# Feed-forward input products of 512 columns, with the last 64 rows of four batches in shared products

## The chip, the cores and the metric

One core of one Trainium2 chip runs the whole program. The metric is the device time of one execution in microseconds (us), as the median of several runs. TensorE is called PE here, VectorE DVE, ScalarE ACT, GpSimd POOL and SyncE SP. Each takes its own instructions in order and waits for the others by semaphores.

## The reference

Eight attention heads for four batches of 576 rows, with a learned bias, feed a gated feed-forward part:

```python
scores = scale * q @ k.T + bias            # bias from log distances, a small two-layer net
attn = exp(scores - max); attn /= sum + 1e-09
x = (attn @ v)                             # per batch 576 x 512 (8 heads of 64)
h = np.maximum(x @ w_in, 0.0)              # 512 -> 1024
conv_out = sum of conv_w[k] * h shifted by k-1 rows, k = 0, 1, 2
gate = 1.0 / (1.0 + np.exp(-conv_out))
out = h * gate @ w_out                     # 1024 -> 512
```

## The kernel before

The attention part (about the first 280 us) goes through 16 pairs of heads and batches, `seq`, with the pair of heads as the outer loop and the batch as the inner one. Its result stands transposed in `xb[b]`: 128 partitions (features of one pair) by 4 pairs by 576 rows. The last pair of all is the fourth of batch 3 (n = 15). The sums of its softmax go from SBUF through DRAM back to all partitions (`store_sums`, `spread_sums`, tile `rb`, both issued by POOL), and `apply_norm` on POOL (L511) multiplies them in.

The feed-forward part works with numbers split into two parts, a rounded high one and the rest (`split_x`, L133 and L134 on POOL), so that each product of matrices is three products: high by high, high by low, low by high. `x_parts(b, c)` splits the quarter c of `xb[b]` into the tile `xs`; `wi` holds w_in and `wo` w_out in the same form. The rows of a batch are columns of the products.

`ffn_in(b, f)` (L529 to L549) makes the hidden features 128 f to 128 f + 127 of batch b: 4 quarters by 3 products by two halves of 288 columns, 24 matmuls at L536, into one of two PSUM tiles (`psS`), from which ACT takes the positive part into `h` (L548). Then four stages follow for each f: `tap` (the middle weight of the convolution; on ACT at L763 for batch 0, on DVE at L761 for the others), `conv` (two DVE instructions at L768), `gate` (a tanh on ACT at L774, then DVE at L775), and `g_parts` (ACT rounds the high part at L90, DVE subtracts for the low part at L788; 512 columns go to a tile `g`, the last 64 to `gt[f]`, which two batches share). The stages are laid out as a pipeline of sets: set j holds conv of f = j-1, gate of j-2, g_parts of j-3 and tap of j. In the loop over `steps` the set j is written right behind `ffn_in(b, j)`, and three more sets drain the pipe. So the first gate of a batch is written behind f = 2.

After the eight f of a batch, `x_parts(b + 1, c)` is written, held back by a dependency until DVE has done the low part of f = 6 (`gated[b, FC - 2]`). Then `ffn_out` (L793) multiplies by w_out: for each f four row tiles of 128 rows, 3 products of 512 columns each, 12 matmuls. For batches 1 and 3 a fifth group does the 64 last rows of two batches together from `gt`, in batch 3 as two halves of 256 columns. In batch 3 the f from 4 on are done row tile by row tile, so that tiles can be stored one by one.

The products for f = 0 and 1 of batch 0 are placed between the last attention units. `wo` for f = 6 and 7 is made in the feed-forward part: DVE and ACT narrow the raw 64-bit words (L99, L101, L105), POOL splits them.

Between engines the order of writing is the order of each engine's queue; nothing reorders it.

Of the kernel before, what the change touches and what calls it, by code (L numbers as in the profile page):

```python
# [9 lines left out]
F32 = mybir.dt.float32  # L10
F32R = mybir.dt.float32r
# [8 lines left out]
def attention_ffn_kernel(  # L20
# [35 lines left out]
    def halves(ap):  # L56
        return ap.rearrange("p (a b) -> p a b", a=2)
# [11 lines left out]
    psum = {"s": psE, "tp": psB, "o": psB}  # L69
    raw_p = pool(ctx, "raw", 2)  # L70
    w_p = pool(ctx, "w", KC + 1)
    x_p = pool(ctx, "x", B)
    e_p = pool(ctx, "e", 2)
    woe_p = pool(ctx, "woe", 1)
    FE = 6

    ident = const.tile([P, P], F32, name="ident")
# [59 lines left out]
    with tc.manual_schedule():  # L137
# [55 lines left out]

        SW = 2 * (S + 32)
        ybuf = [w_p.tile([P, 3, S], F32, name=f"y{i}", tag="w") for i in range(KC)]
        x0 = x_p.tile([P, NP, S], F32, name="x0", tag="x")
        y3 = x_p.tile([P, 4, S], F32, name="y3", tag="x")
        tl = x_p.tile([P, SW + tabs.shape[1]], F32, name="tl", tag="x")
        st1 = x_p.tile([P, SW], F32, name="st1", tag="x")
# [111 lines left out]
        pty_p = pool(att, "pty", 1)  # L311
        sm_p = pool(att, "sm", 4)
        r_p = pool(att, "r", 2)
        rb_p = pool(att, "rb", 1)

        rr_t = [vz_p.tile([P, P], F32, name=f"rr{i}") for i in range(2)]
        for r in rr_t:
# [201 lines left out]
        def x_parts(b, c):  # L519
            if c % 2 == 0:  # L520
                xss["raw"] = raw_p.tile([P, 2, 2, S], F32R, name="xs", tag="raw")
            xs = xss["raw"][:, c % 2]
            first = split_x(xs, xb[b][:, c])
            if b and c == 0:
                tc.add_manual_dep(first.ins, gated[b - 1, FC - 2].ins.name, mybir.DependencyInfo(
                    mybir.DependencyClass.Sync, mybir.DependencyReason.DATA))
            xss[b, c] = xs

        def ffn_in(b, f):  # L529
            ps = psS.tile([P, 2, 512], F32, name="s")  # L530
            cs = slice(f * P, f * P + P)
            i = 0
            for c in range(KC):
                for pw, px in ((0, 0), (0, 1), (1, 0)):
                    for a in range(2):
                        nc.tensor.matmul(  # L536
                            ps[:, a, 0:HS],
                            wi[c][:, pw, cs],
                            xss[b, c][:, px, a * HS:(a + 1) * HS],
                            start=(i == 0),  # L540
                            stop=(i == 3 * KC - 1),
                        )
                    i += 1
            if (b, f) in ((0, 0), (0, 1)):
                h = e_p.tile([P, S], F32, name="h")
            else:
                h = g_p[0].tile([P, S], F32, name="h", tag="g")
            nc.scalar.activation(halves(h), ps[:, :, 0:HS], AF.Relu)  # L548
            return h  # L549

        cwr = []

# [16 lines left out]

        def load_wo(f):  # L570
            if not raw_o:
                raw_o.append(x_p.tile([P, 2, DM, 2], I32, name="raw_o", tag="x"))
            load_w(raw_o[0][:, f % 2], w_out[f * P:(f + 1) * P, :])

        conv_weights = {68: load_conv, 71: narrow_conv, 73: turn_conv}
# [84 lines left out]
        for u, (n, t) in enumerate(flat):  # L660
# [29 lines left out]
            del spt[n, t]  # L690
            if u + 2 >= NU:
                f = u + 2 - NU
                hs_ff[0, f] = ffn_in(0, f)
            if u in (2, 4) or n > 1 and ui == 2 and n + 2 < NSEQ:
                load(n + 2 if n > 1 else 2 + u // 4)
            if u in conv_weights:
# [44 lines left out]
        apply_norm(NSEQ - 2)  # L741
        store_sums(NSEQ - 1)
        spread_sums(NSEQ - 1)
        apply_norm(NSEQ - 1)
        att.close()


# [1 line left out]
        wo_p = pool(ff, "wo", 1)  # L749
        g_p[0] = pool(ff, "g", FC + 4)  # L750
        e2_p = pool(ff, "e2", 2)
        wc_p = pool(ff, "wc", 2)
        o_p = pool(ff, "oo", 3)

        wo += [wo_p.tile([P, 2, DM], F32R, name=f"wo{f}") for f in range(FE, FC)]
# [67 lines left out]
            if k == 3:  # L823
                g_parts(b, f, cvs.pop((b, f)))

        for i, (b, f) in enumerate(steps):
            if b == 0 and f in (2, 4):
                c = FE - 1 + f // 2
                split_w(wc_p, wo[c], raw_o[0][:, c % 2])
            if (b, f) not in hs_ff:  # L830
                hs_ff[b, f] = ffn_in(b, f)
            for k in (1, 2, 3, 0):
                if k <= f:
                    stage(i - k, k)
            if f < FC - 1:
                continue
            for j in range(3):
                for k in (1, 2, 3):
                    if k > j:
                        stage(i + 1 + j - k, k)  # L840
            for c in range(KC):
                if b + 1 < B:
                    x_parts(b + 1, c)
            po = [psT.tile([P, 512], F32, name="tp") for _ in range(3)]
            po.append(psO.tile([P, 512], F32, name="o"))
            lhs = [
                lambda f, gi, t=t: gs[b, f][:, gi, t * P:(t + 1) * P] for t in range(NT)
            ]
            both = FC if b + 1 < B else FC // 2
            for f in range(both):  # L850
                for t in range(NT):
                    ffn_out(po[t], lhs[t], [f])
            for t in range(NT):
                ffn_out(po[t], lhs[t], range(both, FC))
                store(po[t], out[b, t * P:(t + 1) * P, :], t % 2)
            if b % 2:

                nh = 1 if b + 1 < B else 2
                for k in range(nh):
                    cs = slice(k * DM // nh, (k + 1) * DM // nh)  # L860
                    pt = psT.tile([P, 512], F32, name="tp")[:, 0:DM // nh]
                    ffn_out(pt, lambda f, gi: gt[f][:, gi], range(FC), cs)
                    store(pt, out[b - 1:b + 1, NM:, cs], k)
# [82 lines left out]
```

## Time and profile before

| what | value |
|---|---|
| median of 3 runs | 491.34 us (490.48 to 491.41) |
| the profiled execution: its time | 491.75 us |
| the profiled execution: its span | 489.9 us |
| PE busy | 474.1 us, 97% |
| DVE, ACT, POOL busy | 364.3, 311.8, 147.8 us |
| mean granted clock of PE | 0.996 of 2.4 GHz |

The span is the time from the first to the last instruction of the profiled execution; its time holds 1.85 us more. A row of the timeline gives the start and the length of a group of instructions of one kind, and in square brackets the time the engine sat idle ahead of it and what ended that. Matmuls overlap: the length of one is longer than the distance from one to the next, and the distance is what counts in a sum.

### The profile page before, as it was taken

To read this page: it belongs to the slowest core of one execution; us is meant where nothing else is said; L and a number is where in the kernel's file an instruction comes from. 1 tells how busy PE (TensorE), PEld (TensorE's weight loads), DVE (VectorE), ACT (ScalarE), POOL (GpSimd) and SP (SyncE) were. 2 spreads that over 40 slices of the span, in tenths; PEclk is the share of its full clock that TensorE was granted. 3 is DMA by queue.
4 is the path that set the end of the run, shared out by engine and by line. 5 is a ranking of instruction groups with operands and counts; after the bars stand their busy time and mean duration, and the time that the engine had idled before them with its cause. 6 is when DMAs were issued, how large, how long until landed. Compare 5 with 4: busy or idle time off the path is not lost.

```text
span 489.9 us, 11074 instructions
## 1 busy us (share of the span) xinstructions
PE 474.1 (97%) x4202; PEld 352.5 (72%) x4202; DVE 364.3 (74%) x871; ACT 311.8 (64%) x751; POOL 147.8 (30%) x215
## 2 busy tenths in 40 slices
PE   6988899999999999999999999999999999999996
PEld 4333356666666666666666789889988999899986
DVE  6999976788898889988898729944891279438930
ACT  5999886898888889888888836712550145124510
POOL 1000001355445835465457725160007000600000
PEclk9989999999999999999999999999999999999999
DMA  1899857598668795579751300002000200020011
GB/s 37 229 340 301 339 161 164 138 271 221 158 183 208 218 249 156 159 208 272 211 131 50 111 26 26 2 0 87 0 1 1 107 1 1 1 86 1 1 44 64
DMA packets 32584, 60.82 MB, mean 124 GB/s; under 512 B 7196, under 2 KB 15796, under 8 KB 32532
## 3 DMA queue, kind: packets, MB, share of 16 engines
q1 hardware_dynamic: 27380, 47.02, 33.0%
q0 software_dynamic: 4768, 12.77, 9.0%
q8 instruction: 33, 0.54, 0.5%
q10 hardware_dynamic: 384, 0.35, 0.2%
q14 instruction: 19, 0.16, 0.1%
HBM read 44.12 MB, written 15.98 MB: 123 GB/s over the span
## 4 chain that ended last, share of the span: by engine, by line
PE 85%; DVE 0%; issue 0%; DVEq 0%
PE s L536 21%; PE o L471 18%; PE s L363 16%; PE tp L793 16%; PE tp L434 9%; PE o L793 4%; PE s L422 1%; PE s L426 0%; DVE pty L93 0%; DVE sp L374 0%; DVE o L801 0%; PE tp L491 0%; DVE ptx L93 0%; PE tp L565 0%; DVEq L801 0%
## 5 line engine op out<-in xcount | busy, mean ns | idle before, releaser
L374 DVE CUSTOM_DVE_ANT_0 sp<-s,bt 128x576 f32<-128x576 f32 x144 | 103.9, 753 | 30.0 <-PE s L363 12.2
L388 ACT ACTIVATE sp<-sp,nm 128x576 f32<-128x576 f32 x144 | 109.9, 767 | 0.0
L536 PEld LDWEIGHTS s<-xs,wi 128*128 128x128 f32 x768 | 102.8, 189 | 1.2 <-issue 0.5
L536 PE MATMUL s<-xs,wi 128*128 128x288 f32 x768 | 103.6, 296 | 0.0
L363 PE MATMUL s<-qk 64*128 64x288 f32 (+1 forms) x640 | 93.0, 431 | 2.8 <-DVE nm L374 2.1
L363 PEld LDWEIGHTS s<-qk 64*128 64x128 f32 (+1 forms) x640 | 46.8, 175 | 44.3 <-DVE nm L374 15.1
L793 PE MATMUL tp<-wo,g 128*128 128x512 f32 x288 | 70.1, 389 | 0.0
L434 PE MATMUL tp<-identr,sr 64*128 64x64 f32 x1184 | 64.3, 247 | 1.8 <-ACT sp L388 1.8
L793 PEld LDWEIGHTS tp<-wo,g 128*128 128x128 f32 x288 | 53.8, 188 | 11.0
L434 PEld LDWEIGHTS tp<-identr,sr 64*128 64x128 f32 x1184 | 55.6, 136 | 8.0 <-ACT sp L388 2.4
L548 ACT ACTIVATE h<-s 128x576 f32<-128x576 f32 x32 | 20.9, 652 | 55.2 <-PE s L536 55.1
L768 DVE SCALAR_TENSOR_TENSOR cv<-h,cw,cv 128x575 f32<-128x575 f32 x64 | 52.6, 821 | 2.5 <-ACT cv L763 0.6
L250 DVE TENSOR_SCALAR y<-tl,inv,nb 128x576 f32<-128x576 f32 (+33 forms) x112 | 47.6, 498 | 0.1
L471 PE MATMUL o<-ptx,vt 128*64 128x320 f32 x300 | 46.8, 442 | 0.0
L267 PE MATMUL s<-y,pars 128*32 128x512 f32 (+8 forms) x352 | 43.0, 530 | 1.3 <-DVE y L250 0.7
L471 PE MATMUL o<-pty,vt 128*64 128x256 f32 x320 | 44.2, 393 | 0.0
L133 POOL TENSOR_SCALAR xs<-x 128x576 fp32r<-128x576 f32 x16 | 11.9, 743 | 94.9 <-DVE gt L788 94.8
L803 ACT ACTIVATE o<-tp 128x512 f32<-128x512 f32 (+1 forms) x10 | 5.8, 577 | 51.7 <-PE tp L793 51.7
L498 POOL DMA_DIRECT2D r_d<-rt x16 | 10.0, 625 | 87.5 <-DVE rt L93 87.5
L267 PEld LDWEIGHTS s<-y,pars 128*32 128x32 f32 x352 | 16.5, 118 | 25.2 <-DVE y L250 8.2
L801 DVE TENSOR_SCALAR o<-tp 128x512 f32<-128x512 f32 (+1 forms) x5 | 3.2, 638 | 39.6 <-PE tp L793 39.6
L93 DVE COPY ptx<-tp 128x256 f32<-128x256 f32 (+1 forms) x64 | 32.0, 499 | 0.6 <-PE tp L434 0.4
(83 smaller groups left out, 666.1 us busy)
## 6 DMA issues: line engine op xcount, KB each, us to landing
qk<-in_qk_dram SPq DMA_DIRECT2D x32, 320.0 KB, 5.2
bias_d<-st SPq DMA_DIRECT2D x13, 607.0 KB, 5.8
bt<-bias_d POOLq DMA_DIRECT2D x24, 288.0 KB, 6.5
qk<-in_qk_dram SPq DMA_DIRECT2D x32, 144.0 KB, 5.5
rb<-r_d POOLq DMA_DIRECT2D x32, 144.0 KB, 3.2
vt<-in_v_dram SPq DMA_DIRECT2D x16, 256.0 KB, 6.0
raw_w<-in_moe_w_in_dram SPq DMA_DIRECT2D x16, 256.0 KB, 4.7
out_dram<-o SPq DMA_DIRECT2D x16, 256.0 KB, 2.0
```

What stands on the lines that cost most here:

```text
L93: nc.vector.tensor_copy(o, i)
L250: nc.vector.tensor_scalar(y, dist[:, 0:n], inv[:, ig:ig + 1], nb1, op0=ALU.mult, op1=ALU.max)
L267: nc.tensor.matmul(ps[32 * j:32 * j + 32, a // 512 if n > 512 else blk % 2, 0:min(n - a, 512)], w2b, ys[j][:, a:min(n, a + 512)], start=Tr ...
L363: nc.tensor.matmul(ps[po, a, 0:HS], qt[rows, qo:qo + po.stop - po.start], qt[rows, KO + hh * HS:KO + hh * HS + HS], start=True, stop=True,)
L374: nc.vector.tensor_tensor_reduce(out=halves(spt[n, t][0][:, h]), in0=ps[:, :, 0:HS], in1=halves(bt[:, h]), op0=ALU.add, op1=ALU.min, scale ...
L388: exps[n, t, h] = nc.scalar.activation(sp[:, h], sp[:, h], AF.Exp, bias=nm[:, h:h + 1], scale=-1.0, accum_out=sms[n][:, col:col + 1],)
L434: tr = nc.tensor.transpose(ps[a][:, TL * s:TL * s + TL].bitcast(F32R), spf[ra, j:j + P], identr[ra, ra])
L471: nc.tensor.matmul(po[D * h:D * h + D, 0:width], vt[:, slot, :], pt[:, blk, :], start=(c == 0), stop=(c == 4),)
L536: nc.tensor.matmul(ps[:, a, 0:HS], wi[c][:, pw, cs], xss[b, c][:, px, a * HS:(a + 1) * HS], start=(i == 0), stop=(i == 3 * KC - 1),)
L548: nc.scalar.activation(halves(h), ps[:, :, 0:HS], AF.Relu)
L768: nc.vector.scalar_tensor_tensor(out=cv[:, o:o + S - 1], in0=h[:, i:i + S - 1], scalar=cw[:, f, kk:kk + 1], in1=cv[:, o:o + S - 1], op0=AL ...
L793: nc.tensor.matmul(ps, lhs(f, gi), wo[f][:, wj, cs], start=(f == 0 and i == 0), stop=(f == FC - 1 and i == 2),)
```

## The change

The input products of a batch take its first 512 rows in one product instead of 576 rows in two halves. The last 64 rows of all four batches are gathered in a tile `xr` (quarter, high or low, batch, row), and `ffn_rest` makes one product of 256 columns for all of them. These pooled products are written in batch 0, behind its own wide products: f = 6, then pooled 0, f = 7, pooled 1, and then the pooled ones in pairs. ACT takes the 64 columns of batch 0 into `h` and the 192 columns of the others into `hr[f]`; in batches 1 to 3 it copies 64 columns from `hr[f]` into `h`. `x_rest(0)` fills `xr` by DVE from `xs`, `x_rest(1..3)` by POOL from `xb[b]`; for batch 3 that is behind `apply_norm` of the last pair, which moves behind the split of `wo` for f = 6 and two of these. The sets of the gate pipeline of batch 0 are written behind the pooled products (`run`); in batches 1 to 3 three sets go with four f, so that the first gate is written behind f = 3. In batch 3 the row tiles part at f = 6 instead of 4. Some tiles change their pools.

```diff
         def x_parts(b, c):
...
+            n = NM if b else S
             xs = xss["raw"][:, c % 2]
-            first = split_x(xs, xb[b][:, c])
+            first = split_x(xs[:, :, 0:n], xb[b][:, c, 0:n])
...
+        def x_rest(b):
+
+            if b == 0:
+                for k in range(2):
+                    dve(xr[0][:, 2 * k:2 * k + 2, :, 0], xss[0, "pair", k][:, :, :, NM:])
+                return
+            x, hi, lo = xb[b][:, :, NM:], xr[0][:, :, 0, b], xr[0][:, :, 1, b]
+            nc.gpsimd.tensor_scalar(hi, x, 1.0, 0.0, op0=ALU.mult, op1=ALU.add)
+            nc.gpsimd.tensor_sub(lo, x, hi.bitcast(F32))
+
+        xr, hr = [], []
+
+        def in_products(ps, f, rhs):
             i = 0
             for c in range(KC):
                 for pw, px in ((0, 0), (0, 1), (1, 0)):
-                    for a in range(2):
-                        nc.tensor.matmul(
-                            ps[:, a, 0:HS],
-                            wi[c][:, pw, cs],
-                            xss[b, c][:, px, a * HS:(a + 1) * HS],
-                            start=(i == 0),
-                            stop=(i == 3 * KC - 1),
-                        )
+                    nc.tensor.matmul(
+                        ps, wi[c][:, pw, f * P:f * P + P], rhs(c, px), start=(i == 0), stop=(i == 3 * KC - 1)
+                    )
                     i += 1
+
+        def ffn_in(b, f, ps=None):
+
+            if ps is None:
+                ps = psS.tile([P, 2, 512], F32, name="s")
+            in_products(ps[:, 0], f, lambda c, px: xss[b, c][:, px, 0:NM])
...
-            nc.scalar.activation(halves(h), ps[:, :, 0:HS], AF.Relu)
-            return h
+            nc.scalar.activation(h[:, 0:NM], ps[:, 0], AF.Relu)
+            if b:
+                act(h[:, NM:], hr[f][:, b - 1])
+            hs_ff[b, f] = h
+
+        def ffn_rest(ps, f):
+            in_products(ps[:, 0:B * TL], f, lambda c, px: xr[0][:, c, px].rearrange("p b s -> p (b s)"))
+            nc.scalar.activation(hs_ff[0, f][:, NM:], ps[:, 0:TL], AF.Relu)
+            nc.scalar.activation(hr[f].rearrange("p b s -> p (b s)"), ps[:, TL:B * TL], AF.Relu)
...
         spread_sums(NSEQ - 1)
-        apply_norm(NSEQ - 1)
         att.close()
...
-        for i, (b, f) in enumerate(steps):
-            if b == 0 and f in (2, 4):
-                c = FE - 1 + f // 2
-                split_w(wc_p, wo[c], raw_o[0][:, c % 2])
-            if (b, f) not in hs_ff:
-                hs_ff[b, f] = ffn_in(b, f)
-            for k in (1, 2, 3, 0):
-                if k <= f:
-                    stage(i - k, k)
-            if f < FC - 1:
-                continue
-            for j in range(3):
-                for k in (1, 2, 3):
-                    if k > j:
-                        stage(i + 1 + j - k, k)
+        def run(b, sets):
+            for j in sets:
+                for k in (1, 2, 3, 0):
+                    if 0 <= j - k < FC:
+                        stage(b * FC + j - k, k)
+
+        hr += [hr_p.tile([P, B - 1, TL], F32, name=f"hr{f}") for f in range(FC)]
+        ws = [narrow(tp, raw_o[0][:, k], ("cv", "cv")) for k, tp in enumerate((e_p, e2_p))]
+        xr.append(xa_p.tile([P, KC, 2, B, TL], F32R, name="xr", tag="x"))
+        x_rest(0)
+        split_x(wo[FE], ws[0])
+        for b in range(1, B):
+            if b == B - 1:
+                apply_norm(NSEQ - 1)
+            x_rest(b)
+        split_x(wo[FE + 1], ws[1])
+
+        for b in range(B):
+            if b == 0:
+                for f in range(2, 6):
+                    ffn_in(0, f)
+                for j, todo in enumerate(((6, None, 0), (7, None, 1), (None, 2, 3), (None, 4, 5), (None, 6, 7))):
+                    main, *rest = todo
+                    ps = psS.tile([P, 2, 512], F32, name="s")
+                    if main is not None:
+                        ffn_in(0, main, ps)
+                    for k, f in enumerate(rest):
+                        if f is not None:
+                            ffn_rest(ps[:, k], f)
+                    run(0, [j])
+                done = 5
+            else:
+                done = 0
+                for f in range(FC):
+                    ffn_in(b, f)
+                    upto = (3 * f + 1) // 4 + 1
+                    run(b, range(done, upto))
+                    done = upto
+            run(b, range(done, FC + 3))
...
-            both = FC if b + 1 < B else FC // 2
+            both = FC if b + 1 < B else 3 * FC // 4
```

PE's queue before, from the last input products of batch 0 (f = 7) into its first output products; `s` is the PSUM tile, `wi_751` to `wi_754` are the four quarters of w_in:

```order
L536 MATMUL s<-xs,wi_751 128x288 x6
L536 MATMUL s<-xs,wi_752 128x288 x6
L536 MATMUL s<-xs,wi_753 128x288 x6
L536 MATMUL s<-xs,wi_754 128x288 x6
L793 MATMUL tp<-wo_755,g 128x512 x9
L793 MATMUL o<-wo_755,g 128x512 x3
```

PE's queue of the change at the same place, from the products of f = 6 on; the rows with `xr` are pooled products, and six more such groups (f = 2 to 7) follow the last row:

```order
L548 MATMUL s<-xs,wi_757 128x512 x3
L548 MATMUL s<-xr,wi_754 128x256 x3
L548 MATMUL s<-xr,wi_755 128x256 x3
L548 MATMUL s<-xr,wi_756 128x256 x3
L548 MATMUL s<-xr,wi_757 128x256 x3
L548 MATMUL s<-xs,wi_754 128x512 x3
L548 MATMUL s<-xs,wi_755 128x512 x3
L548 MATMUL s<-xs,wi_756 128x512 x3
L548 MATMUL s<-xs,wi_757 128x512 x3
L548 MATMUL s<-xr,wi_754 128x256 x3
L548 MATMUL s<-xr,wi_755 128x256 x3
```

Six matmuls of 288 columns for a quarter have become three of 512, and eight groups of twelve with 256 columns stand between the inputs of batch 0 and its outputs.

POOL's queue before, behind the issue of the last `rb`; `x_1535` is batch 3, `wo_4535` and `wo_4536` are f = 6 and 7, `x_957` is batch 1:

```order
L504 DMA rb<-r_d 64x576 x2
L511 TENSOR_TENSOR x_1535<-x_1535,rb 128x576
L133 TENSOR_SCALAR wo_4535<-w 128x512
L134 TENSOR_TENSOR wo_4535<-w,wo_4535 128x512
L133 TENSOR_SCALAR wo_4536<-w 128x512
L134 TENSOR_TENSOR wo_4536<-w,wo_4536 128x512
L133 TENSOR_SCALAR xs<-x_957 128x576
```

The same place of the change; `x_960`, `x_1289` and `x_1538` are batches 1, 2 and 3:

```order
L505 DMA rb<-r_d 64x576 x2
L135 TENSOR_SCALAR wo_4512<-w 128x512
L136 TENSOR_TENSOR wo_4512<-w,wo_4512 128x512
L539 TENSOR_SCALAR xr<-x_960 128x4x64
L540 TENSOR_TENSOR xr<-x_960,xr 128x4x64
L539 TENSOR_SCALAR xr<-x_1289 128x4x64
L540 TENSOR_TENSOR xr<-x_1289,xr 128x4x64
L512 TENSOR_TENSOR x_1538<-x_1538,rb 128x576
L539 TENSOR_SCALAR xr<-x_1538 128x4x64
L540 TENSOR_TENSOR xr<-x_1538,xr 128x4x64
L135 TENSOR_SCALAR wo_4513<-w 128x512
L136 TENSOR_TENSOR wo_4513<-w,wo_4513 128x512
```

Six instructions now stand between the last issue and the last `apply_norm`: the split of `wo` for f = 6 (two) and the parts of batches 1 and 2 (four). The parts of batch 3 come behind it.

ACT's queue of the change from pooled f = 2 on (before, each `h` of 576 columns was followed by one set); L569 and L570 take the pooled products, L794 is the tanh:

```order
L569 ACTIVATE h<-s 128x64
L570 ACTIVATE hr_4524<-s 128x192
L569 ACTIVATE h<-s 128x64
L570 ACTIVATE hr_4525<-s 128x192
L794 ACTIVATE cv<-cv 128x576
L783 ACTIVATE cv<-h,cw 128x576
L569 ACTIVATE h<-s 128x64
L570 ACTIVATE hr_4526<-s 128x192
L569 ACTIVATE h<-s 128x64
L570 ACTIVATE hr_4527<-s 128x192
L794 ACTIVATE cv<-cv 128x576
L92 ACTIVATE g<-cv 128x512
```

The first tanh (f = 0) stands behind the four ACT instructions of pooled f = 2 and 3, the second (f = 1) behind those of f = 4 and 5.

## Rows read from the trace of the kernel before

**Rows 1.** The page, busy time of each engine
```profile
PE 474.1 (97%) x4202; PEld 352.5 (72%) x4202; DVE 364.3 (74%) x871; ACT 311.8 (64%) x751; POOL 147.8 (30%) x215
```

**Rows 2.** Who waited for whom, 291.6 to 486 us: total us, times, longest
```profile
POOL xs L133 <- DVE gt L788: 94.8, 3, 43.8
```

**Rows 3.** The chain that ended last, 250 to 490 us: start, us, what
```profile
332.83 25.58 PE s L536 x192
...
361.16 2.04 PE tp L793 x9
...
480.37 5.76 PE tp L793 x48
```

**Rows 4.** Timeline of PE: start, us, form of the matmuls, count
```profile
291.63 19.42 PE L536 MATMUL s<-xs,wi 128*128 128x288 f32 x144
310.89 2.23 PE L793 MATMUL tp<-wo,g 128*128 128x512 f32 x9
...
480.21 5.91 PE L793 MATMUL tp<-wo,gt 128*128 128x256 f32 x48
```

**Rows 5.** Timeline of POOL, end of attention and between batches
```profile
261.55 0.40 POOL L133 TENSOR_SCALAR wo<-wu 128x256 fp32r<-128x256 f32 x1 [2.82 <-DVE wu L105]
...
262.72 1.42 POOL L511 TENSOR_TENSOR x<-x,rb 128x576 f32<-128x576 f32 x1
...
295.23 1.08 POOL L504 DMA_DIRECT2D rb<-r_d  x2 [1.60 <-DMA r_d<-rt]
298.81 1.88 POOL L511 TENSOR_TENSOR x<-x,rb 128x576 f32<-128x576 f32 x1 [2.50 <-DMA rb<-r_d]
300.67 1.12 POOL L133 TENSOR_SCALAR wo<-w 128x512 fp32r<-128x512 f32 x1
301.87 1.61 POOL L134 TENSOR_TENSOR wo<-w,wo 128x512 fp32r<-128x512 f32 x1
...
367.69 1.03 POOL L133 TENSOR_SCALAR xs<-x 128x576 fp32r<-128x576 f32 x1 [36.16 <-DVE gt L788]
...
370.20 0.68 POOL L133 TENSOR_SCALAR xs<-x 128x576 fp32r<-128x576 f32 x1
...
372.35 0.67 POOL L133 TENSOR_SCALAR xs<-x 128x576 fp32r<-128x576 f32 x1
```

**Rows 6.** Timeline of ACT: small pieces, a tanh, and a first `h`
```profile
291.66 0.38 ACT L90 ACTIVATE x<-o 128x256 f32<-128x256 f32 x1 [1.67 <-PE o L471]
...
299.93 0.24 ACT L90 ACTIVATE gt<-cv 128x64 fp32r<-128x64 f32 x1
...
336.05 0.65 ACT L548 ACTIVATE h<-s 128x576 f32<-128x576 f32 x1 [3.26 <-PE s L536]
...
343.00 0.68 ACT L774 ACTIVATE cv<-cv 128x576 f32<-128x576 f32 x1
```

**Rows 7.** Timeline of DVE: one set of batch 0, then one of batch 1
```profile
308.93 1.66 DVE L768 SCALAR_TENSOR_TENSOR cv<-h,cw,cv 128x575 f32<-128x575 f32 x2
310.51 0.75 DVE L775 SCALAR_TENSOR_TENSOR cv<-cv,h 128x576 f32<-128x576 f32 x1
311.17 0.68 DVE L788 TENSOR_TENSOR g<-cv,g 128x512 fp32r<-128x512 f32 x1
...
311.91 1.67 DVE L768 SCALAR_TENSOR_TENSOR cv<-h,cw,cv 128x575 f32<-128x575 f32 x2
...
348.32 0.52 DVE L761 TENSOR_SCALAR cv<-h,cw 128x576 f32<-128x576 f32 x1
...
351.87 0.52 DVE L761 TENSOR_SCALAR cv<-h,cw 128x576 f32<-128x576 f32 x1
```

**Rows 8.** Early attention: PE's timeline, then windows (us, PE, PEld, DVE, ACT, POOL busy, PEclk)
```profile
27.39 0.59 PE L434 MATMUL tp<-identr,sr 64*128 64x64 f32 x10 [1.78 <-ACT sp L388]
...
28.00:29.00 1.00, 1.00 (x12) 0.51 (x16) 1.00 (x4) 1.00 (x4) 0.00 (x0) 0.71 1.05 408
...
30.00:31.00 1.00, 1.00 (x8) 0.52 (x8) 1.00 (x4) 1.00 (x3) 0.00 (x0) 0.50 1.03 391
```

More of the change, by code (lines that the diff above doesn't have):

```diff
@@ L71, in attention_ffn_kernel @@
     w_p = pool(ctx, "w", KC + 1)
-    x_p = pool(ctx, "x", B)
+    xa_p = pool(ctx, "xa", 1)
+    x_p = pool(ctx, "x", B - 1)
     e_p = pool(ctx, "e", 2)
     woe_p = pool(ctx, "woe", 1)
+    rb_p = pool(ctx, "rb", 1)
     FE = 6
@@ L195, in attention_ffn_kernel @@
         ybuf = [w_p.tile([P, 3, S], F32, name=f"y{i}", tag="w") for i in range(KC)]
-        x0 = x_p.tile([P, NP, S], F32, name="x0", tag="x")
+        x0 = xa_p.tile([P, NP, S], F32, name="x0", tag="x")
         y3 = x_p.tile([P, 4, S], F32, name="y3", tag="x")
@@ L313, in attention_ffn_kernel @@
         r_p = pool(att, "r", 2)
-        rb_p = pool(att, "rb", 1)
         rr_t = [vz_p.tile([P, P], F32, name=f"rr{i}") for i in range(2)]
@@ L527, in x_parts @@
             xss[b, c] = xs
-        def ffn_in(b, f):
-            ps = psS.tile([P, 2, 512], F32, name="s")
-            cs = slice(f * P, f * P + P)
+            xss[b, "pair", c // 2] = xss["raw"]
+        def x_rest(b):
[8 more added lines that the diff above has]
+        def in_products(ps, f, rhs):
             i = 0
@@ L571, in load_wo @@
             if not raw_o:
-                raw_o.append(x_p.tile([P, 2, DM, 2], I32, name="raw_o", tag="x"))
+                raw_o.append(xa_p.tile([P, 2, DM, 2], I32, name="raw_o", tag="x"))
             load_w(raw_o[0][:, f % 2], w_out[f * P:(f + 1) * P, :])
@@ L692, in attention_ffn_kernel @@
                 f = u + 2 - NU
-                hs_ff[0, f] = ffn_in(0, f)
+                ffn_in(0, f)
             if u in (2, 4) or n > 1 and ui == 2 and n + 2 < NSEQ:
@@ L751, in attention_ffn_kernel @@
         e2_p = pool(ff, "e2", 2)
-        wc_p = pool(ff, "wc", 2)
+        hr_p = pool(ff, "hr", 1)
         o_p = pool(ff, "oo", 3)
@@ L824, in stage @@
                 g_parts(b, f, cvs.pop((b, f)))
-        for i, (b, f) in enumerate(steps):
-            if b == 0 and f in (2, 4):
-                c = FE - 1 + f // 2
-                split_w(wc_p, wo[c], raw_o[0][:, c % 2])
-            if (b, f) not in hs_ff:
-                hs_ff[b, f] = ffn_in(b, f)
-            for k in (1, 2, 3, 0):
-                if k <= f:
-                    stage(i - k, k)
-            if f < FC - 1:
-                continue
-            for j in range(3):
-                for k in (1, 2, 3):
-                    if k > j:
-                        stage(i + 1 + j - k, k)
+        def run(b, sets):
[16 more added lines that the diff above has]
+                for f in range(2, 6):
+                    ffn_in(0, f)
+                for j, todo in enumerate(((6, None, 0), (7, None, 1), (None, 2, 3), (None, 4, 5), (None, 6, 7))):
[16 more added lines that the diff above has]
+            run(b, range(done, FC + 3))
             for c in range(KC):
```

## Prediction

> **What bounds the kernel now.** Read the page first: PE is busy 97% of the span [rows 1]. Then the waits of the feed-forward part: in 194 us no row has PE waiting for another engine, and the longest wait is POOL's, for DVE [rows 2]. Then the chain that ended last: from 291 us on it is matmuls end to end [rows 3]. So what counts here is the distance from one matmul to the next, and a wait that is put in front of one.
>
> The chain gives that distance for three widths [rows 3], and the timeline the widths [rows 4]. 288 columns: 25.58 us / 192 = 133.2 ns. 512 columns: 2.04 us / 9 = 226.7 ns. 256 columns: 5.76 us / 48 = 120.0 ns. At 2.4 GHz the columns alone are 120.0, 213.3 and 106.7 ns, so each matmul costs some 13.3 ns beside its columns, whatever its width.
>
> **The products.** The columns stay the same: 768 x 288 = 384 x 512 + 96 x 256 = 221,184. The matmuls fall from 768 to 480. In batches 1 to 3 the inputs go from 25.58 to 96 x 0.2267 = 21.76 us, 3.82 us less each. Batch 0 takes all pooled products: 21.76 + 96 x 0.1200 = 33.28 us, 7.70 us more. Together 7.70 - 11.46 = **-3.76 us**, all of it on the path, if PE stays without waits. That is the gain; the rest of this part asks which waits appear.
>
> The TensorE page of the Trainium skill (TensorE: Matmul & The Clock Gate, section "Wait - 56ns, not 53.3ns?") gives a fixed cost of about 2.5 ns per warm matmul. By that, 288 matmuls fewer would be worth 0.72 us. The three rows show five times that, and in this kernel's own form, each matmul with a weight load of its own; I take the rows.
>
> **Wait 1, the last norm.** The first pooled product needs all four batches' last 64 rows, also those of the last pair. PE's side: f = 0 and 1 lie ahead of the rest of batch 0 and save 24 x 133.2 - 12 x 226.7 ns = 0.48 us each, so f = 2 starts at 291.63 - 0.95 = 290.68 [rows 4]; five wide f (2 to 6) of 2.72 us follow, and the first pooled product could start at 304.28. POOL's side: its chain hangs on PE's transpose of the sums, so it also comes 0.95 earlier: the issue of `rb` ends at 295.36 and `rb` is there at 297.86 [rows 5]. New ahead of the norm are the split of `wo` 6 and the parts of batches 1 and 2, behind it that of batch 3. A split of 256 columns takes 262.72 - 261.55 = 1.17 us [rows 5], the same element count as `xr`'s 4 x 64. One of 576 columns takes 372.35 - 370.20 = 2.15 us, so 512 columns lie at 1.95 by the line between. The sum: 295.36 + 1.95 + 1.17 + 1.17 = 299.65 (`rb` is there), norm 1.42, parts of batch 3 1.17: 302.24. That is 2.0 us ahead of PE: no wait. Upper end: everything at the prices seen under collision with DVE, 2.81 for `wo` (300.67 to 303.48), 1.88 for the norm, and 2.15 for each `xr`, if the 64-element pieces cost like 576 columns: 306.5, a wait of 2.2 us. I take the lower one, because DVE has little to do then: its first convolution waits for a pooled product. The narrowing of both raw `wo` on DVE and ACT is done by 294, ahead of POOL's need, and costs nothing. The norm and the parts of batch 3 now also hold up `wo` 7, which PE needs some 30 us later.
>
> **Wait 2, the first gates of batch 0.** Pooled f = 0 ends at 305.7, f = 7 at 308.4, pooled 1 at 309.9, and pooled 2 to 7 take 1.44 us each: the outputs could start at 318.5 (before: 310.89). The gates cannot start before the pooled products, since a convolution needs the last 64 columns too. The latest link is ACT: its tanh for f = 1 stands behind the pooled pieces of f = 4 and 5. Pooled 5 ends at 315.64; plus about 0.2 us to reach ACT, pieces of 64 and 192 columns at 0.24 and at most 0.38, and 0.68 for the tanh [rows 6], less 0.1 of overlap: 317.0. DVE then has the gate of f = 1 (0.66 to the next start) and the low part of f = 0 (0.68) [rows 7]: 318.3, as the outputs start. From there DVE runs without gaps, one set in 311.91 - 308.93 = 2.98 us [rows 7], while PE uses up one f in 12 x 226.7 = 2.72 us. The low part of f = 5, five sets on, is there at 333.2; PE needs it for the third product of f = 5, at 318.5 + 5 x 2.72 + 0.45 = 332.55. With 0.1 us for the semaphore PE waits **0.75 us** in all. After that DVE has no more convolutions, and f = 6 and 7 come in 1.4 us and less. If the small pieces take twice as long, 1.2 us are lost; at half of everything, 0.5.
>
> **Wait 3, batches 1 to 3.** Now T is the start of the inputs. DVE needs 351.87 - 348.32 = 3.55 us for a set [rows 7], PE only 2.72 for an f, so in ACT's queue a tanh that waits for DVE would hold up the `h` behind it. The later gates prevent that. The last tanh ahead of the free run, f = 3, stands behind `h` 7: T + 21.76 + 0.2 + 0.65 + 0.24 + 0.68 less overlaps, T + 23.3 [rows 6]. The low part of f = 2 follows at T + 24.7, that of f = 5 three sets later, at T + 35.3; PE needs it at T + 21.76 + 13.60 + 0.45 = T + 35.8. Margin 0.5: nothing lost. The copies from `hr` (0.24 each on ACT) lie beside matmuls: ACT sat idle for 3.26 us ahead of the first `h` of batch 1 [rows 6].
>
> **Wait 4, the split of the next batch.** POOL starts when f = 6 is done, about T + 37.0, and needs 2.51 for its first quarter (late start under DVE) and 2.15 for the others [rows 5] at 576 columns: 8.96; at 512, by the line above, 8.2: T + 45.2. PE needs the last low part ten products into the next batch, at T + 43.5 + 2.27 = T + 45.8 (after batch 1 another 5.44 later). After batch 0 the margin is as small: f = 6 is done at 334.7, the split at 343.0, PE is there at 318.5 + 0.75 + 21.76 + 2.27 = 343.3. So nothing lost; at the full price of 576, 0.6 and 0.3 us.
>
> In batch 3 the row tiles that part at f = 6 come 1.36 us apart instead of 2.72, and so do their stores; the 48 last products of 256 columns stay behind them for 5.8 us and hide that: nothing. SP's queue is unchanged.
>
> **The sum**: -3.76 + 0.75 + 0.1 for signals = -2.9 us against the profiled execution's 491.75, that is 488.85. The median of the runs lies 0.41 lower, so I forecast **488.4**. A measurement can tell about 0.2%, 1.0 us, from no change.
>
> **Rivals.**
> POOL dearer than a line between two rows (at 512 columns or in strided pieces): waits 1 and 4 open partly. The price is 0.6 + 0.3 us for the split of the next batch, and up to 1.5 us at the norm: 489.3 to 490.8. For it: margins of 0.3 to 0.6 us. 20%.
>
> The norm comes late and PE's clock falls, the slower side. Place: ahead of the first pooled product. It decides if POOL finishes batch 3's parts after 304.3. At the upper prices the wait is 2.2 us. After a wait of 1.78 us early in the kernel the granted clock fell: 0.71 in the next full slice of 1 us and then 0.50, the level of 1.2 GHz [rows 8]; some 3 us of it cost 1.5. Then -2.9 + 2.2 + 1.5 = +0.8, and with the 0.9 of wait 4, which the same prices bring, +1.7: 493.0. Against it: 2 us of margin, and DVE idle. 8%.
>
> The 13.3 ns do not go with the matmul but with something that stays, so the gain is 0.7 us at most. Then -0.7 + 0.75 = 0: 491.4. Against it: three widths on one line. This is the page's rule above, taken as the result. 5%.
>
> No waits at all, if ACT or DVE reach the first gates sooner: 491.34 - 3.76 = 487.6 to 488. 12%.
>
> **How the numbers follow.** My forecast has 55%, with 487.9 to 489.2 as its own range. The range 487.5 to 490.4 adds the case without waits and the dearer POOL. Faster by over 1.0 us: the forecast, no waits, and most of the dear POOL, 0.82. Within: the rest of that and the fixed price, 0.10. Slower: the late norm, 0.08.
>
> **What would show it.** Input products 226.7 ns apart and pooled ones 120.0; the inputs of batches 1 to 3 in 21.8 us; outputs of batch 0 that start at about 318.5 and last 22.5 us instead of 21.8; POOL done with `xr` by 302 to 303; a granted clock of 1.00 throughout the feed-forward part. A gap of PE ahead of the first pooled product, or input products of 512 columns well under 226 ns apart, would prove me wrong.

## The result, and the profile after

The change made the kernel slower. Its median was 493.9 us (493.14 to 495.36, 4 runs) against 491.37 for the kernel before on the same chip: a ratio of 1.0056, with a 95% interval of 1.0039 to 1.0074. On a second chip, with 12 runs, it was 493.62 against 491.35: 1.0040, interval 1.0026 to 1.0053. Forecast were 488.4 us and faster.

The page, busy time of each engine (answers to [rows 1]):

```profile
PE 472.3 (96%) x3914; PEld 332.2 (67%) x3914; DVE 361.2 (73%) x873; ACT 316.9 (64%) x791; POOL 147.4 (30%) x221
```

PE has 288 instructions fewer and is busy 1.8 us less, yet the span grew from 489.9 to 493.6 us: so PE stands idle somewhere. Who waited for whom from 291 to 490 us (answers to [rows 2]; total us, times, longest):

```profile
PE s L548 <- ACT hr L570: 2.5, 3, 1.3
...
PE s L548 <- POOL wo L136: 0.7, 1, 0.7
PE s L548 <- ACT h L562: 0.7, 1, 0.7
```

Where the feed-forward part had no row with PE waiting for another engine, it now has three, five waits in all, each ahead of an input product. The timeline of PE shows their places (answers to [rows 4]; start, us, form, count, and in brackets the idle time ahead):

```profile
292.13 13.89 PE L548 MATMUL s<-xs,wi 128*128 128x512 f32 x60
306.76 1.66 PE L548 MATMUL s<-xr,wi 128*128 128x256 f32 x12 [0.73 <-POOL wo L136]
308.26 2.91 PE L548 MATMUL s<-xs,wi 128*128 128x512 f32 x12
311.85 3.13 PE L548 MATMUL s<-xr,wi 128*128 128x256 f32 x24 [0.69 <-ACT h L562]
315.52 3.14 PE L548 MATMUL s<-xr,wi 128*128 128x256 f32 x24 [0.53 <-ACT hr L570]
319.33 3.14 PE L548 MATMUL s<-xr,wi 128*128 128x256 f32 x24 [0.67 <-ACT hr L570]
323.80 1.69 PE L548 MATMUL s<-xr,wi 128*128 128x256 f32 x12 [1.33 <-ACT hr L570]
325.32 2.23 PE L813 MATMUL tp<-wo,g 128*128 128x512 f32 x9
...
347.79 21.97 PE L548 MATMUL s<-xs,wi 128*128 128x512 f32 x96
369.60 2.20 PE L813 MATMUL tp<-wo,g 128*128 128x512 f32 x9
```

The waits stand ahead of pooled 0, 1, 3, 5 and 7: always ahead of the second product in a shared `s` tile (f = 6 and pooled 0, f = 7 and pooled 1, pooled 2 and 3, 4 and 5, 6 and 7). Pooled 2, 4 and 6 follow without idle time, inside the groups of 24. The idle times sum to 3.95 us. From start to start more is lost, 5.2 us as the experiments below show: a matmul of 512 columns lasts 0.39 us at a distance of 0.227, and behind a gap this overlap of some 0.16 us is gone too. Five times that is 0.8 us; the other 0.4 stay open.

The timeline of ACT at two of these places:

```profile
306.06 0.60 ACT L562 ACTIVATE h<-s 128x512 f32<-128x512 f32 x1 [2.12 <-PE s L548]
...
318.94 0.34 ACT L570 ACTIVATE hr<-s 128x192 f32<-128x192 f32 x1
```

The read of f = 6 ends at 306.66 and pooled 0 starts at 306.76. The read of pooled 4 ends at 319.28 and pooled 5 starts at 319.33. So the second product of a tile starts right behind ACT's read of the first. For pooled 0 the profile names POOL's split of `wo` 7 instead, which ended at 306.04; that label has to be tested.

The chain of work shows why the last of the waits is the longest (start, us, what):

```profile
321.20 0.31 ACT hr L570
321.51 0.57 ACT cv L794
322.08 0.52 ACT g L92
322.60 0.14 ACT gt L92
322.75 0.66 ACT cv L783
323.41 0.11 ACT h L569
323.52 0.23 ACT hr L570
323.75 0.04 issue
323.80 1.69 PE s L548 x12
```

Pooled 6 had ended at 322.47 (319.33 + 3.14), but its two reads (L569, L570) stand in ACT's queue behind a whole set of the gates (tanh, high parts, tap) and end at 323.75. Between the pairs before, the sets were shorter: a tap alone ahead of pooled 3 (0.53 us of waiting), a tanh and a tap ahead of pooled 5 (0.67).

PE's start-to-start times, from its timelines, put the whole difference together. The forecast's column is worked from its own steps:

| stretch | before | forecast | after |
|---|---|---|---|
| f = 0 to f = 2 of batch 0 | 11.25 | 10.30 | 10.36 |
| f = 2 to the first output product | 19.26 | 27.82 | 33.19 |
| outputs of batch 0 | 21.78 | 22.51 | 22.47 |
| inputs of batch 1 | 25.59 | 21.76 | 21.81 |
| inputs of batch 2, and of batch 3 | 25.58 each | 21.76 each | 21.76 each |

Against before, after stands at -0.89 + 13.93 + 0.69 - 3.78 - 3.82 - 3.82 = +2.31 us from f = 0 on. Every line but the second is as forecast; that one is 5.4 us too long. In the profiled execution f = 0 also began 1.39 us later than before (281.77 against 280.38). Both together are the 3.7 us between the spans.

### The profile page after: what moved, and what is told of

Its sections match the earlier page's. It is cut to its first block, busy times and chain, and to the rows that moved or that the text cites. A ratio compares the mean times of both kernels' runs of the same rounds, so it can differ in the third digit from the quotient of the medians.

```text
span 493.6 us, 10553 instructions
## 1 busy us (share of the span) xinstructions
PE 472.3 (96%) x3914; PEld 332.2 (67%) x3914; DVE 361.2 (73%) x873; ACT 316.9 (64%) x791; POOL 147.4 (30%) x221
## 4 chain that ended last, share of the span: by engine, by line
PE 81%; POOL 2%; ACT 1%; issue 1%; DVE 0%; DMA 0%; POOLq 0%; DVEq 0%; ACTq 0%
PE o L472 17%; PE s L548 17%; PE s L364 16%; PE tp L813 16%; PE tp L435 9%; PE o L813 4%; PE s L423 1%; DMA r_d<-rt 0%; POOL xr L540 0%; POOL x L512 0%; POOL wo L136 0%; PE s L427 0%; ACT cv L783 0%; POOL wo L135 0%; ACT hr L570 0%
## 5 line engine op out<-in xcount | busy, mean ns | idle before, releaser
L548 PE MATMUL s<-xs,wi 128*128 128x512 f32 x384 | 88.6, 390 | 0.0
L548 PEld LDWEIGHTS s<-xs,wi 128*128 128x128 f32 x384 | 71.8, 188 | 15.9 <-issue 0.5
L562 ACT ACTIVATE h<-s 128x512 f32<-128x512 f32 x32 | 19.1, 598 | 57.3 <-PE s L548 57.3
L135 POOL TENSOR_SCALAR xs<-x 128x512 fp32r<-128x512 f32 (+1 forms) x16 | 11.3, 708 | 111.3 <-DVE gt L808 111.2
L795 DVE SCALAR_TENSOR_TENSOR cv<-cv,h 128x576 f32<-128x576 f32 x32 | 24.1, 754 | 18.8 <-ACT cv L794 18.8
L794 ACT ACTIVATE cv<-cv 128x576 f32<-128x576 f32 x32 | 21.8, 681 | 21.8 <-DVE cv L788 21.8
L269 PEld LDWEIGHTS s<-y,pars 128*32 128x32 f32 x352 | 15.2, 115 | 26.1 <-DVE y L252 11.5
```

The costliest lines, as they stand in the source:

```text
L269: nc.tensor.matmul(ps[32 * j:32 * j + 32, a // 512 if n > 512 else blk % 2, 0:min(n - a, 512)], w2b, ys[j][:, a:min(n, a + 512)], start=Tr ...
L548: nc.tensor.matmul(ps, wi[c][:, pw, f * P:f * P + P], rhs(c, px), start=(i == 0), stop=(i == 3 * KC - 1))
L795: nc.vector.scalar_tensor_tensor(out=cv, in0=cv, scalar=1.0, in1=h, op0=ALU.add, op1=ALU.mult)
```

## The experiments

Three theories of the five waits. **A**: the tile is what the program orders by. The second product of a tile is written after ACT's read of the first has been written, so PE waits for that read, though it writes the other half of the tile (`ps[:, 1]`, not `ps[:, 0]`). **B**: two `s` tiles are too few, and PE waits for a tile to come free. **C**: the first of the waits is for POOL's split of `wo` 7, as the profile names it. The queue of PE, listed with the engines that each instruction waits for, speaks for A. First the change, pooled 0 and pooled 1; below it pooled 0 and 1 with a tile for each pooled product:

```
L548 MATMUL s<-xr,wi_754 128x256 [waits DVE_49,Activation_49,Pool_49]
...
L548 MATMUL s<-xr,wi_754 128x256 [waits Activation_49]

L548 MATMUL tp<-xr,wi_754 128x256 [waits DVE_49,Pool_49]
...
L548 MATMUL tp<-xr,wi_754 128x256 x3
```

**Same tiles, reads last.** Both products of a tile are written first, and ACT's reads of both behind them. Tiles, their number and POOL's queue stay as in the change.

```diff
                     if main is not None:
-                        ffn_in(0, main, ps)
+                        ffn_in(0, main, ps, rest[1])
+                    else:
+                        for k, f in enumerate(rest):
+                            rest_products(ps[:, k], f)
                     for k, f in enumerate(rest):
                         if f is not None:
-                            ffn_rest(ps[:, k], f)
+                            rest_relu(ps[:, k], f)
```

Here `ffn_in` calls `rest_products` for the pooled product that it is given ahead of its own read.

> Same PSUM tiles and the same products in the same order; ACT's reads of a tile are written behind both products of that tile instead of between them. Theory A (the second product of a tile waits for ACT's read of the first, since both lie in one tile): the five waits of PE in batch 0 go; from f = 2 to the first output product 27.8 us instead of 33.2, and 488.5 to 489.0 us in all (493.9 less 5.3, plus 0.1 for later reads). Theory B (two tiles are too few, PE waits for a free one): the waits stay at other products, 492.5 or more. Theory C (ahead of the first pooled product PE waits for POOL's split of wo 7): four waits go, one of 0.7 stays, 489.4.

Measured: 489.25 us (487.96 to 491.61, 12 runs), against before 0.9952, interval 0.9934 to 0.9969. PE's timeline:

```profile
305.70 1.59 PE L548 MATMUL s<-xr,wi 128*128 128x256 f32 x12
307.13 2.91 PE L548 MATMUL s<-xs,wi 128*128 128x512 f32 x12
309.88 10.23 PE L548 MATMUL s<-xr,wi 128*128 128x256 f32 x84
319.95 2.23 PE L817 MATMUL tp<-wo,g 128*128 128x512 f32 x9
```

All five waits are gone, with the same two tiles, so B falls. The one ahead of pooled 0 is gone too, with POOL's queue untouched, so C falls. POOL's timeline of this run says so directly:

```profile
304.56 1.29 POOL L136 TENSOR_TENSOR wo<-w,wo 128x512 fp32r<-128x512 f32 x1
```

That split ends at 305.85, and pooled 0 has started at 305.70 without waiting for it. The outputs start 319.95 - 291.96 (f = 2) = 27.99 us after f = 2; forecast were 27.82.

**A tile for each pooled product.** The reads stay where they are; only the tile is another.

```diff
-                    ps = psS.tile([P, 2, 512], F32, name="s")
                     if main is not None:
-                        ffn_in(0, main, ps)
+                        ffn_in(0, main)
                     for k, f in enumerate(rest):
                         if f is not None:
-                            ffn_rest(ps[:, k], f)
+                            ffn_rest(psT.tile([P, 512], F32, name="tp"), f)
```

> Each pooled product gets a PSUM tile of its own (from the three that the outputs use later); ACT's reads stay where they were. Theory A: the same as with the reads behind, 27.8 us from f = 2 to the first output product and 488.5 to 489.0 us. Theory B: also faster, since there are more tiles, 488.5 to 489.5; so this run does not tell A from B, the one with the reads behind does. If ACT's place in its queue were the cause (tanh and tap ahead of a read), the waits of 0.5 to 1.3 us would stay: 492.5.

Measured: 488.48 us (487.97 to 489.3, 6 runs), 0.9925, interval 0.9902 to 0.9947. PE's timeline:

```profile
304.14 1.60 PE L548 MATMUL tp<-xr,wi 128*128 128x256 f32 x12
305.57 2.91 PE L548 MATMUL s<-xs,wi 128*128 128x512 f32 x12
308.32 10.24 PE L548 MATMUL tp<-xr,wi 128*128 128x256 f32 x84
318.39 2.23 PE L813 MATMUL tp<-wo,g 128*128 128x512 f32 x9
```

Again no idle time, and 27.99 us from f = 2 (290.40). ACT's queue is in the order of the change, so that order alone does not make PE wait. Two edits that share only the parting of read and write in a tile take the same waits away: A is shown. Their price in the change is 33.19 - 27.99 = **5.20 us**. The outputs of batch 0 take 22.57 us here, with DVE's late gates still in them, as forecast.

**Reads last, with early gates in batches 1 to 3** (`upto = f + 1`, one set behind each f as before the change). The forecast held that a tanh that waits for DVE would hold up the `h` behind it, and that the later gates prevent that.

> The reads behind both products as in the first run, and in batches 1 to 3 the first gate behind f = 2 as before the change. The step of the prediction on the later gates: a tanh that waits for DVE holds up the positive part behind it and PE runs out of PSUM tiles: 0.5 to 1.5 us more than the first run, with waits of PE at f = 6 or 7. Rival: the two tiles cover it, as ACT's tanh waits under 1 us for DVE at f = 7: same time as the first run within 0.3 us, no waits of PE.

Measured: 488.44 us (487.99 to 489.39, 6 runs), 0.9926, interval 0.9904 to 0.9949. PE has no wait in batches 1 to 3, and their inputs take 21.80 us and less. ACT's timeline at f = 7 of batch 1:

```profile
363.95 0.69 ACT L798 ACTIVATE cv<-cv 128x576 f32<-128x576 f32 x1 [0.63 <-DVE cv L792]
```

ACT does wait for DVE, but only 0.63 us and behind the last `h`. So the later gates are not needed to keep PE supplied with inputs.

**A set behind each pooled product.** As with own tiles, but pooled 2 to 7 are written one by one, with a set each: the first gates come sooner.

```diff
-                for j, todo in enumerate(((6, None, 0), (7, None, 1), (None, 2, 3), (None, 4, 5), (None, 6, 7))):
-                    main, *rest = todo
+                for j, main in enumerate((6, 7) + 6 * (None,)):
...
-                    for k, f in enumerate(rest):
-                        if f is not None:
-                            ffn_rest(psT.tile([P, 512], F32, name="tp"), f)
-                    run(0, [j])
-                done = 5
+                    ffn_rest(psT.tile([P, 512], F32, name="tp"), j)
+                    run(0, [j] if j < 6 else [])
+                done = 6
```

> Own PSUM tiles, and the pooled products of f = 2 to 7 one by one with one set of the gates behind each, so that the tanh of f = 1 stands behind pooled f = 3 instead of 5. Theory A with the prediction's second wait (DVE's first gates set when the low part of f = 5 is there, 0.75 us): that wait goes too, outputs of batch 0 in 21.8 us, 0.7 us below the run with own tiles: 487.7 to 488.3 us. If the gates are set by something else (DVE's 2.98 us per set from the first output on): no change against own tiles.

Measured: 489.57 us (488.65 to 490.57, 9 runs), 0.9949, interval 0.9931 to 0.9968. DVE's late gates no longer hold up the outputs, but PE's timeline has a new wait inside them:

```profile
320.24 1.66 PE L813 MATMUL tp<-wo,g 128*128 128x512 f32 x6 [1.41 <-ACT hr L570]
```

The three PSUM tiles go round, so the first three output row tiles get those of pooled 5, 6 and 7. The wait is ahead of the second row tile (the first three products start at 317.97), and what it waits for is the read of pooled 6 in ACT's timeline:

```profile
319.87 0.32 ACT L570 ACTIVATE hr<-tp 128x192 f32<-128x192 f32 x1
```

It ends at 320.19, since it now stands behind two more sets than with own tiles. (The expectation of the mixed tiles below puts the wait down to the tile of pooled 7 alone; it was that of pooled 6.) The outputs of batch 0 take 23.51 us instead of 22.57: the gain was more than given back by a wait for a tile.

**The change once more**, on one chip with the next three.

> The change itself once more, beside the others on one chip, since its first comparison had four runs and its profiled execution came to the feed-forward part 1.39 us later than that of before. If the later start is part of the change, f = 0 starts at 281 to 282 us again and the time stays 2.5 us above before. If it only differs from execution to execution (279.3 to 281.6 in the four other kernels with the same attention part), the change is at 492 to 493, some 3.5 to 5 us above the version with a tile for each pooled product, which is what its five waits of 5.3 us in batch 0 cost. In either case the outputs of batch 0 start some 33.2 us after f = 2.

Measured: the 493.62 us told above, a little over the expected 493. f = 0 starts at 280.00 and the outputs of batch 0 at 323.54, 33.18 us after f = 2 (290.36). So the five waits come again with the same price, and the late start of f = 0 is no part of the change. From f = 0 to the end of the span it takes 211.8 us again, 2.3 more than before (489.9 - 280.38 = 209.5), which is the distance of the medians.

**Halves.** To price a matmul by itself: own tiles, but each wide product is two of 256 columns, the same columns in 384 matmuls more.

```diff
-            in_products(ps[:, 0], f, lambda c, px: xss[b, c][:, px, 0:NM])
+            HN = NM // 2
+            i = 0
+            for c in range(KC):
+                for pw, px in ((0, 0), (0, 1), (1, 0)):
+                    for a in range(2):
+                        nc.tensor.matmul(
+                            ps[:, a, 0:HN], wi[c][:, pw, f * P:f * P + P],
+                            xss[b, c][:, px, a * HN:(a + 1) * HN], start=(i == 0), stop=(i == 3 * KC - 1)
+                        )
+                    i += 1
```

> The version with a tile for each pooled product, but each wide input product is two of 256 columns: 384 matmuls more, the same columns. If each matmul costs 13.3 ns beside its columns, the inputs of a batch take 192 x 0.1200 = 23.04 us instead of 21.76, and the time is 488.5 + 5.1 = 493.6 us. By the 2.5 ns of the Trainium skill (TensorE: Matmul & The Clock Gate) it would be 0.24 us for a batch and 489.4 in all.

Measured: 493.74 us (492.93 to 495.04, 12 runs), 1.0047, interval 1.0032 to 1.0061. PE's timeline:

```profile
341.52 23.20 PE L562 MATMUL s<-xs,wi 128*128 128x256 f32 x192
364.55 2.23 PE L823 MATMUL tp<-wo,g 128*128 128x512 f32 x9
```

A batch takes 23.03 us for its inputs (expected 23.04) and the whole 5.3 us more than with own tiles (expected 5.1). The 13.3 ns go with the matmul.

**Mixed tiles.** Own tiles, with sets as soon as their pooled product is there, and with the output's tiles kept free.

```diff
-                for j, todo in enumerate(((6, None, 0), (7, None, 1), (None, 2, 3), (None, 4, 5), (None, 6, 7))):
-                    main, *rest = todo
-                    if main is not None:
-                        ffn_in(0, main)
-                    for k, f in enumerate(rest):
-                        if f is not None:
-                            ffn_rest(psT.tile([P, 512], F32, name="tp"), f)
-                    run(0, [j])
+                for f, sets in enumerate(((0,), (1,), (2,), (), (3,), (), (4,), ())):
+                    if f < 2:
+                        ffn_in(0, 6 + f)
+                    if f < 3:
+                        ps = psT.tile([P, 512], F32, name="tp")
+                    elif f == 3:
+                        ps = psO.tile([P, 512], F32, name="o")
+                    else:
+                        ps = psS.tile([P, 2, 512], F32, name="s")[:, 0]
+                    ffn_rest(ps, f)
+                    run(0, sets)
```

> As the version with a tile for each pooled product, but the sets of the gates are written as soon as the pooled product they need (behind pooled 0, 1, 2, 4 and 6), and the pooled products 3 to 7 take the tiles that the outputs do not need first, so that no output tile waits for the read of pooled 7. If DVE's late first gates are what is left in batch 0 (0.7 to 1.1 us) and the wait of 1.41 us with a set behind each pooled product came from the tile of pooled 7 alone, both are gone: outputs 28.0 us after f = 2 and 21.8 long, 0.8 us less than with own tiles, 487.7. If the sets between the pooled products delay ACT's reads by themselves, PE waits ahead of a pooled product by 0.5 to 1.5 us: 488.5 to 489.5.

Measured: 487.94 us (487.34 to 488.86, 6 runs), 0.9921, interval 0.9900 to 0.9941. PE's timeline:

```profile
318.65 2.23 PE L813 MATMUL tp<-wo,g 128*128 128x512 f32 x9
...
340.44 21.92 PE L548 MATMUL s<-xs,wi 128*128 128x512 f32 x96
```

The outputs of batch 0 take 340.44 - 318.65 = 21.79 us and no longer wait for DVE; no row has PE waiting after 291 us. From f = 0 (280.17) to the end of the span (486.2) it is 206.0 us, 5.8 less than the change. This is the fastest version in the study; against own tiles the intervals overlap, and only the traces tell the two apart.

**Reads last, parting at 4.** In batch 3 the row tiles part at f = 4 again (`both = FC if b + 1 < B else FC // 2`), an edit that the forecast costed at nothing.

> The version with both products of a tile written ahead of ACT's reads, but in batch 3 the row tiles part at f = 4 again, as before the change. The prediction costed that edit at nothing, since the 48 last products of 256 columns hide the stores: then it is the 489.25 us of that version, within 0.5. If the later parting lets the stores crowd at the end or makes a product wait, this one differs by 1 us or more.

Measured: 491.6 us (490.61 to 493.71, 12 runs), 1.0004, interval 0.9988 to 1.0021: the whole gain is gone. PE's timeline, outputs of batch 3:

```profile
455.94 2.20 PE L817 MATMUL tp<-wo,g 128*128 128x512 f32 x9
...
469.53 0.96 PE L817 MATMUL tp<-wo,g 128*128 128x512 f32 x3 [1.42 <-DVE g L812]
470.94 8.26 PE L817 MATMUL tp<-wo,g 128*128 128x512 f32 x28 [0.44 <-DVE g L812]
479.04 2.88 PE L817 MATMUL o<-wo,g 128*128 128x512 f32 x12
481.76 5.91 PE L817 MATMUL tp<-wo,gt 128*128 128x256 f32 x48
```

Windows of the same stretch (us, busy time of PE, PEld, DVE, ACT, POOL, then PEclk, DMA share, GB/s):

```profile
468.00:472.00 4.00, 2.14 (x7) 1.38 (x7) 3.81 (x9) 2.16 (x5) 0.00 (x0) 0.90 0.00 0
472.00:476.00 4.00, 4.00 (x13) 3.16 (x13) 0.00 (x0) 0.60 (x1) 0.00 (x0) 0.67 0.18 70
...
472.00:473.00 1.00, 1.00 (x3) 0.74 (x3) 0.00 (x0) 0.17 (x1) 0.00 (x0) 0.50 0.00 0
```

Parted at 4, the first row tile asks for f = 5 to 7 before the other row tiles have used f = 4, and with later gates DVE does not have them yet. Two waits of 1.86 us in all follow, and then the granted clock falls: it is 0.67 on average over 4 us and 0.50, its level of 1.2 GHz, from 472 to 473: 28 products take 479.04 - 470.94 = 8.10 us instead of 28 x 0.2267 = 6.35. The outputs of batch 3 take 25.82 us instead of 21.76. This execution, at 493.28 us, is the second slowest of the twelve. The two fastest, at 490.61 and 490.62, had a mean granted clock of 1.000 and still lie 2.65 us above the fastest with reads last alone (487.96). So most of the 2.35 us between the medians is probably the two waits, with the fall of the clock on top in some executions; no trace of one without the fall was taken.

**Mixed tiles, early gates, parting at 4**: nothing is left of the changed gates and parting of batches 1 to 3.

```diff
-                    upto = (3 * f + 1) // 4 + 1
+                    upto = f + 1
...
-            both = FC if b + 1 < B else 3 * FC // 4
+            both = FC if b + 1 < B else FC // 2
```

> The version with mixed tiles, with early gates in batches 1 to 3 (one set behind each f) and the row tiles of batch 3 parting at f = 4, so that of the changed order of the gates and the parting nothing is left. With later gates the parting at 4 cost two waits for DVE of 1.42 and 0.44 us in the outputs of batch 3 and a fall of the clock. If those come from the later gates, they are gone: with early gates the low part of f = 5 is done 9.83 us after the first output product of batch 3, against the 12.0 us at which PE wants it here, and f = 7 at 12.0 against 13.4. Then the outputs of batch 3 take 21.76 us and the time is 487.9 us, that of the mixed tiles, within 0.5. If the parting at 4 costs something by itself, the same two waits or a fall of the clock stand in batch 3 again, and the time is 489.5 to 492.

Measured: 488.08 us (487.12 to 489.34, 6 runs), 0.9930, interval 0.9910 to 0.9950: the time of the mixed tiles. PE's timeline, outputs of batch 3:

```profile
455.08 2.20 PE L813 MATMUL tp<-wo,g 128*128 128x512 f32 x9
...
476.84 5.91 PE L813 MATMUL tp<-wo,gt 128*128 128x256 f32 x48
```

They take 21.76 us, without a wait. So the parting at 6 only makes up for the later gates: the gates and the parting of the kernel before do as well.

## Why the prediction was wrong

The step that failed is the row of times in wait 2: "Pooled f = 0 ends at 305.7, f = 7 at 308.4, pooled 1 at 309.9, and pooled 2 to 7 take 1.44 us each: the outputs could start at 318.5". It takes all these products back to back, and so puts the wait for a PSUM tile at nothing without a reason. The prediction asked what makes a pooled product's data late (wait 1) and what makes the gates late (wait 2), but never what makes its PSUM tile late. In the change two products share a tile with ACT's read of the first written between them, and the second waits for that read. Reads last and own tiles showed this from two sides, at 5.20 us in place of 0: 1.80 us by the start of pooled 1 (19.72 us after f = 2 against 17.92 with own tiles), the other 3.40 at pooled 3, 5 and 7. No rival held it: the norm's rival had its place ahead of the first pooled product, but for POOL, and the label of that wait even names POOL, wrongly.

The other steps:

- **The products**, -3.76 us: right. 512 columns lie 21.76 / 96 = 226.7 ns apart, and the halves priced the matmul at the same 13.3 ns. The Trainium skill (TensorE: Matmul & The Clock Gate, section "Wait - 56ns, not 53.3ns?") gives some 2.5 ns per warm matmul: by that the halves would have cost 1.0 us (estimate), where 5.3 were measured. The measurement decides, and the rival that the 13.3 ns belong to something else falls.
- **Wait 1**, the last norm, none: right, since the wait that did come ahead of pooled 0 was for ACT's read. The parts of one batch took 1.2 us and a split of 512 columns 2.0, where 1.17 and 1.95 had been reckoned, in POOL's timeline (answers to [rows 5]):

```profile
302.84 0.41 POOL L539 TENSOR_SCALAR xr<-x 128x256 fp32r<-128x256 f32 x1
303.34 0.74 POOL L540 TENSOR_TENSOR xr<-x,xr 128x256 fp32r<-128x256 f32 x1
304.04 0.63 POOL L135 TENSOR_SCALAR wo<-w 128x512 fp32r<-128x512 f32 x1
304.75 1.29 POOL L136 TENSOR_TENSOR wo<-w,wo 128x512 fp32r<-128x512 f32 x1
```

  `xr` is complete at 304.08, and the five wide products end their starts at 292.13 + 60 x 0.2267 = 305.73. Forecast was a lead of 2.0 us, and 1.65 are seen.
- **Wait 2**, DVE's late gates, 0.75 us: right where its products do run back to back, with own tiles. There the low part of f = 0 is ready at 318.12, 0.27 us ahead of the outputs (forecast 0.2), DVE runs without gaps from there, and the outputs take 22.57 us, 0.81 over 96 x 0.2267 = 21.76. That the change itself shows 0.71 is luck. There the low part of f = 0 is ready at 323.47, 1.85 us ahead of the outputs, but then DVE waits for the tanh of f = 2, which stands behind the reads of pooled 7. DVE's timeline, own tiles and then the change:

```profile
317.44 0.68 DVE L808 TENSOR_TENSOR g<-cv,g 128x512 fp32r<-128x512 f32 x1
...
326.58 0.76 DVE L795 SCALAR_TENSOR_TENSOR cv<-cv,h 128x576 f32<-128x576 f32 x1 [1.38 <-ACT cv L794]
```

- **Wait 3**: nothing lost, as forecast, but its reason was not borne out: with early gates nothing is lost either.
- **Wait 4**, the split of the next batch, none: right; the inputs of batches 1 to 3 take 21.76 to 21.81 us.
- **Batch 3's parting at 6**, nothing: right as a term, but not by its reason. That the last products hide the stores is not what counts: with early gates the parting at 4 takes the same time. What the parting at 6 does is keep the later gates from making PE wait; without it the median is 2.35 us higher (491.6 against 489.25).

With the five waits taken away and little else moved, the change lands at 488.48 us (own tiles) and 489.25 (reads last), near the forecast of 488.4. So -2.9 us was the worth of the idea, and +5.2 the price of the tile it was put in.

## What to carry to other kernels

For every product that is added, ask three things: when its inputs are there, when its result is wanted, and when its output tile may be written. If the program orders by tiles, two products that share one with a read written between them run in turn with the reading engine, even in different halves of it. Write both products ahead of the reads, or give each its own tile, and then look at who gets that tile next: the wait of 1.41 us with a set behind each product was the same mistake one step later.

## What had not been expected of the hardware

The five waits, of 0.53 to 1.33 us within 18 us, left the clock alone. Windows of the change (columns as above):

```profile
310.00:320.00 10.00, 8.11 (x59) 7.17 (x58) 4.53 (x7) 4.17 (x12) 0.00 (x0) 1.00 0.00 0
320.00:330.00 10.00, 8.67 (x54) 7.66 (x53) 7.08 (x12) 7.15 (x19) 0.00 (x0) 1.00 0.00 1
```

A wait of 1.42 us went both ways, though in one case another followed. After 1.42 us and, close behind, 0.44 us in the parting at 4, the granted clock was 0.67 over a window of 4 us. After a wait of 1.42 us at 50.29 us in the second profile of the change it stayed at 1.00. In the first profile it was 0.61 and 0.54 in the two windows of 2 us around and after a wait of 2.24 us at 50.69.

And f = 0 of batch 0 began anywhere from 279.3 to 281.8 us in the profiled executions, with the same attention part but for tiles and the place of one norm. A difference of 2 us in a whole time is therefore better read from f = 0 on than from the spans.
